# Running the two 64-row tiles of the TensorE array out of phase, with PSUM in single banks

## The chip, the cores and the metric

The kernel runs on one core of one Trainium2 chip. Times are device microseconds of that core. "Before" is 742.64 us in the median of the three runs (742.42 to 743.63). A ratio is made from the fast runs of both kernels in the same rounds, so it isn't quite the ratio of the medians quoted beside it.

The profile's names: PE is the engine of the matmuls (TensorE) and PEld its weight loads, ACT is ScalarE, DVE VectorE, POOL GpSimd. PSUM is the memory that matmuls write into; it is used here in eight banks, each of 512 fp32 columns.

## The reference

Tokens (32768 of them, 192 features, from 8 sequences) pass through a causal convolution with 7 softmax-normalised taps for each of 8 heads, and then through two matrix products with an ELU between them:

```python
out = np.einsum('hk,bskhg->bshg', softmax(weight), x_unfolded)   # 7 taps per head
h = out.reshape(-1, 192) @ w_in                                  # 192 -> 2048
g = np.where(h > 0.0, h, np.exp(np.minimum(h, 0.0)) - 1.0)       # ELU
return (g @ w_out).astype(np.float32)                            # 2048 -> 192
```

## The kernel before

The work runs in 32 **groups** of 1024 tokens. A group has 16 **places**, one for each 128 of the 2048 hidden features. (I number them 0 to 15, and first products through all groups as n = 16 x group + place.) The array is used as two tiles of 64 rows. Everything is bf16 or fp16 into fp32 PSUM.

- **First product**: at each place, each tile takes three matmuls of 512 columns (192 = 3 x 64) for its 512 tokens, into one PSUM bank.
- **The chain behind it**: ACT takes the exponential of the bank into SBUF (E), POOL clamps it, and DVE combines E and the bank into gT (fp16). Only then is the bank free.
- **Output rounds**: 128-token by 192-column matmuls of gT with w_out. A half group takes 64 pairs of them. Each tile holds 64 of the 128 hidden features of a place, so every output sum (bank `ops[g]`) needs both tiles, first one and then the other. `turned` says which tile works on which sum. The program never lets both tiles write one bank at once: at a **tile change** the new tile waits on a semaphore for the other tile's last round.
- **Conv**: 240-column matmuls for a later group, copied to SBUF by ACT.

Before, both tiles do everything in step, as pairs, and PSUM slots are pairs of banks (three slots for first products and convs, one pair for output sums):

```python
GAPS = ((), (1,), (16,), (7,), (7,), (7,), (6,), (7, 3, 10))   # rounds after each first product; turned flips at each number
...
elif item[0] == "h":                        # one place: both tiles
    wait_slot(k)                            # DVE has combined BOTH banks of the slot's last user
    for j in range(3):
        for r in range(2):
            ins = pe.matmul(H[:, k % 3, GS * r : GS * (r + 1)], w_in[...], att[...],
                            start=(j == 0), stop=(j == 2), tile_position=(HP * r, 0))
    ins.then_inc(s_h)
else:                                       # rounds: both tiles, each on its own sum
    ...
        if runs[prev][0][1] != turned:
            W(s_swap, 2 * (prev + 1))       # tile change
    ...
        for rt in range(2):
            g = rt ^ turned
            ins = pe.matmul(acc[:, g, d0 : d0 + D], gT[HP * rt : HP * (rt + 1), ...], w_out[...],
                            tile_position=(HP * rt, 0))
```

ACT copies output sum 0 and DVE output sum 1 at the end of each half group.

## Time and profile before

| | before |
|---|---|
| median | 742.64 us |
| one group in the middle of the run | 22.40 us |
| the same, if both tiles streamed without a gap | 21.74 us |
| busy: PE, DVE, ACT, POOL | 98, 89, 86, 89% |

The group time is the mean distance of the first first-product of group 3 from that of group 30, over 27 groups. The second row comes from the start times of single matmuls in the trace. Within a tile, a first product follows another after 216 ns, a round after 82.5 ns and a conv matmul after 102 ns. A group has 48, 128 and 8 of them per tile: 10.36 + 10.57 + 0.82 = 21.74 us.

The page of the kernel before, parts 1 and 5 (line, engine, operation, tiles, count | busy us, mean ns | idle time just before, and what ended most of it):

```profile
PE 730.1 (98%) x11866; PEld 502.6 (68%) x11866; DVE 657.3 (89%) x1106; ACT 636.4 (86%) x1224; POOL 663.7 (89%) x1108
...
L583 DVE SCALAR_TENSOR_TENSOR gT<-E,H 128x512 f16<-128x512 f32 x1024 | 622.1, 681 | 68.4 <-POOL E L431 68.1
...
L513 ACT ACTIVATE E<-H 128x512 f32<-128x512 f32 x1024 | 542.9, 602 | 72.2 <-PE H L733 39.3
...
L773 PEld LDWEIGHTS ops<-w_out,gT 64*128 64x128 f16 x8064 | 343.9, 94 | 117.7 <-issue 14.4
...
L733 PEld LDWEIGHTS H<-att,w_in 64*128 64x128 bf16 x3072 | 131.9, 94 | 105.2 <-DVE gT L583 30.6
...
L473 ACT ACTIVATE osb<-ops 128x384 f32<-128x384 f32 x63 | 31.3, 497 | 9.5 <-PE ops L773 9.5
L575 DVE COPY osb<-ops 128x384 f32<-128x384 f32 x63 | 34.6, 549 | 4.6 <-PE ops L773 4.6
```

Who waited for whom from 52 to 697 us, the stretch without start and tail (us in total, times, longest):

```profile
PEld H L733 <- DVE gT L583: 25.4, 58, 0.4
...
PEld ops L773 <- PE ops L773: 7.5, 50, 0.2
```

The windows view of four groups (length, then each engine's busy us):

```profile
core 0: us, PE busy (x) PEld busy (x) DVE busy (x) ACT busy (x) POOL busy (x), PEclk, DMA share, GB/s
300.00:389.60 89.60, 89.60 (x1476) 62.05 (x1472) 81.43 (x136) 79.10 (x153) 82.23 (x138) 1.00 0.47 79
```

PE sets the pace here: it is busy for the whole window, and no other engine is. "Busy" hides the gaps, though. A matmul's recorded end is modelled (243 ns for a round, 376 ns for a first product), so the next one nearly always starts inside it. The single start times give the gaps: 22.40 - 21.74 = 0.66 us a group. They lie where first products wait for DVE to free a slot (0.41 us a group, at places 4, 6, 12, 14 and 0), and where rounds change tiles behind a conv (a step of 151 ns instead of 102; 0.17 us a group). The two lines of the waits view are these two (the view counts from the weight load, and only what the modelled ends leave open, so its sums are smaller).

### The profile page before, as it was taken

The page shows a single profiled execution, that of the slowest core. Times are in us where ns is not written, and L with a number is a line of the kernel's source. Part 1 is how long each engine was busy: PE and PEld are TensorE (multiplying, and loading weights), DVE is VectorE, ACT ScalarE, POOL GpSimd, SP SyncE. Part 2 cuts the span into 40 slices and gives each one's busy share as a digit, 9 for nine tenths or more (in the row PEclk, how much of TensorE's full clock was granted, in tenths as well). Part 3 has the DMA queues.
Part 4 walks back from the last instruction along what each step waited for, and adds up shares of the span by engine and source line. Part 5 has one row for each costly group of instructions (what it writes and reads, how often), then busy time and mean ns, then how long its engine had stood idle before and what let it go on. Part 6 is the DMA issues. An engine that isn't in the chain of part 4 may idle for free.

```text
span 741.6 us, 28196 instructions
## 1 busy us (share of the span) xinstructions
PE 730.1 (98%) x11866; PEld 502.6 (68%) x11866; DVE 657.3 (89%) x1106; ACT 636.4 (86%) x1224; POOL 663.7 (89%) x1108
## 2 busy tenths in 40 slices
PE   8799999999999999999999999999999999999998
PEld 4467666667667667666667666666676676666666
DVE  4889889889889889899899898898898898898895
ACT  5888898888888888888888888888888988988883
POOL 7899999999999999999999999999999999998883
PEclk9999999999999999999999999999999999999999
DMA  9554524544535535435535435545345445343201
GB/s 168 95 85 83 94 43 89 94 67 87 76 58 94 94 60 96 68 62 95 95 61 94 57 75 94 89 65 94 49 83 95 70 84 94 43 88 81 68 24 65
DMA packets 131858, 58.94 MB, mean 79 GB/s; under 512 B 96020, under 2 KB 131348, under 8 KB 131732
## 3 DMA queue, kind: packets, MB, share of 16 engines
q0 software_dynamic: 43136, 17.28, 24.1%
q1 hardware_dynamic: 88308, 39.37, 20.4%
q8 instruction: 93, 1.52, 0.8%
q10 hardware_dynamic: 288, 0.49, 0.2%
q14 instruction: 33, 0.27, 0.2%
HBM read 35.61 MB, written 25.17 MB: 82 GB/s over the span
## 4 chain that ended last, share of the span: by engine, by line
PE 94%; DMA 3%; POOL 1%; ACT 0%; DVE 0%; issue 0%
PE ops L773 45%; PE H L733 45%; PE H L701 3%; DMA w_in<-in_moe_w_in_dram 1%; DMA w_in<-w_in 1%; PE H L773 1%; POOL E L431 1%; POOL w_in L386 1%; POOL xg L381 0%; DVE gT L583 0%; ACT E L513 0%; DMA wh<-in_weight_dram 0%; ACT csb L483 0%; DVE osb L575 0%
## 5 line engine op out<-in xcount | busy, mean ns | idle before, releaser
L583 DVE SCALAR_TENSOR_TENSOR gT<-E,H 128x512 f16<-128x512 f32 x1024 | 622.1, 681 | 68.4 <-POOL E L431 68.1
L431 POOL TENSOR_SCALAR E<-E 128x512 f32<-128x512 f32 x1024 | 603.5, 613 | 65.7 <-ACT E L513 57.8
L513 ACT ACTIVATE E<-H 128x512 f32<-128x512 f32 x1024 | 542.9, 602 | 72.2 <-PE H L733 39.3
L773 PE MATMUL ops<-w_out,gT 64*128 64x192 f16 x8064 | 428.2, 243 | 1.8 <-ACT csb L483 1.2
L773 PEld LDWEIGHTS ops<-w_out,gT 64*128 64x128 f16 x8064 | 343.9, 94 | 117.7 <-issue 14.4
L733 PE MATMUL H<-att,w_in 64*128 64x512 bf16 x3072 | 409.5, 377 | 3.8 <-DVE gT L583 2.1
L733 PEld LDWEIGHTS H<-att,w_in 64*128 64x128 bf16 x3072 | 131.9, 94 | 105.2 <-DVE gT L583 30.6
L483 ACT ACTIVATE csb<-H 128x480 bf16<-128x480 f32 x118 | 60.9, 568 | 12.6 <-PE H L701 12.6
L381 POOL DMA_DIRECT2D xg<-in_x_dram x62 | 55.2, 890 | 0.1
L701 PE MATMUL H<-xg,Tm 64*128 64x240 bf16 x472 | 44.4, 263 | 0.0
L473 ACT ACTIVATE osb<-ops 128x384 f32<-128x384 f32 x63 | 31.3, 497 | 9.5 <-PE ops L773 9.5
L575 DVE COPY osb<-ops 128x384 f32<-128x384 f32 x63 | 34.6, 549 | 4.6 <-PE ops L773 4.6
L701 PEld LDWEIGHTS H<-xg,Tm 64*128 64x128 bf16 x472 | 18.0, 93 | 3.7 <-issue 1.2
L773 PE MATMUL H<-w_out,gT 64*128 64x192 f16 x128 | 5.9, 243 | 0.0
L386 POOL DMA_DIRECT2D w_in<-in_moe_w_in_dram x7 | 4.9, 697 | 0.6 <-DMA wh<-in_weight_dram 0.6
L773 PEld LDWEIGHTS H<-w_out,gT 64*128 64x128 f16 x128 | 5.3, 94 | 0.0
L608 PE MATMUL ops<-zw 128*128 128x512 bf16 x9 | 4.0, 631 | 1.2 <-DVE zw L525 1.2
L483 ACT ACTIVATE csb<-ops 128x480 bf16<-128x480 f32 x6 | 3.5, 588 | 0.0
L608 PEld LDWEIGHTS ops<-zw 128*128 128x128 bf16 x9 | 1.2, 143 | 3.2 <-issue 1.9
L561 DVE CAST att<-H 128x512 bf16<-128x512 f32 x1 | 0.7, 692 | 3.0 <-PE H L664 3.0
L701 PE MATMUL ops<-xg,Tm 64*128 64x240 bf16 x24 | 2.3, 266 | 1.0 <-ACT csb L483 0.8
L701 PEld LDWEIGHTS ops<-xg,Tm 64*128 64x128 bf16 x24 | 0.8, 94 | 2.8 <-ACT csb L483 1.3
(49 smaller groups left out, 30.8 us busy)
## 6 DMA issues: line engine op xcount, KB each, us to landing
out_dram<-osb SPq DMA_DIRECT2D x126, 192.0 KB, 4.8
xg<-in_x_dram POOLq DMA_DIRECT2D x61, 240.0 KB, 5.2
w_in<-in_moe_w_in_dram POOLq DMA_DIRECT2D x4, 192.0 KB, 6.8
w_out<-in_moe_w_out_dram POOLq DMA_DIRECT2D x1, 768.0 KB, 15.1
att<-csb SPq DMA_TRANSPOSE x31, 6.2
xf<-in_x_dram ACTq DMA_DIRECT2D x1, 384.0 KB, 3.2
xf<-in_x_dram SPq DMA_DIRECT2D x1, 384.0 KB, 3.8
w_in<-in_moe_w_in_dram POOLq DMA_DIRECT2D x1, 288.0 KB, 10.9
```

The lines of the kernel that those rows point to most:

```text
L381: g.dma_start(xg[:, b, v0 : v0 + whole, :], src).then_inc(s_x[b][part - 1], 16)
L386: g.dma_start(w_in[HP * r : HP * (r + 1), :, c0:c1], moe_w_in.rearrange("(p j) f -> p j f", j=3)[:, :, c0:c1],).then_inc(s_w[k], 16)
L431: g.tensor_scalar(out=E[:, n % NE, u, :], in0=E[:, n % NE, u, :], scalar1=1.0, scalar2=0.0, op0=ALU.min, op1=ALU.max,).then_inc(s_clp)
L473: a.activation(*out_pieces(key, 0), ACT.Copy).then_inc(s_oev)
L483: return a.activation(csb[:, s % 2, :].rearrange("p (j v h i) -> p h j v i", j=3, v=2 * WPG, h=HEADS)[:, h0 : h0 + HB], conv_bank(m)[:, b, ...
L513: a.activation(E[:, n % NE, u, :], H[:, k, GS * u : GS * (u + 1)], ACT.Exp).then_inc(s_exp)
L575: v.tensor_copy(*out_pieces(key, 1)).then_inc(s_od)
L583: v.scalar_tensor_tensor(out=gT[:, s % NG3, q, u, :], in0=E[:, n % NE, u, :], scalar=1.0, in1=H[:, slot_of_pair[n] % 3, GS * u : GS * (u + ...
L608: pe.matmul(ops[:, 0, :], zw[:, 0:P], zw[:], start=True, stop=True)
L701: ins = pe.matmul(to[:, b, n1 * hh : n1 * (hh + 1)], Tm[HP * rt : HP * (rt + 1), h, :], xg[HP * rt : HP * (rt + 1), s % NXB, :, :].rearran ...
L733: ins = pe.matmul(H[:, k % 3, GS * r : GS * (r + 1)], w_in[HP * r : HP * (r + 1), j, 2 * FC * (q // 2) + q % 2 : 2 * FC * (q // 2 + 1) : 2 ...
L773: ins = pe.matmul(acc[:, g, d0 : d0 + D], gT[HP * rt : HP * (rt + 1), t % NG3, q, g, t0 : t0 + P], w_out[HP * rt : HP * (rt + 1), q, :], s ...
```

## The change

The intent: use banks one by one instead of in pairs, and let one tile do its first product while the other does rounds, so that banks are asked for, filled and freed evenly. The order is planned: each tile gets its own list with planned times (216, 83 and 236 ns per item), and the two lists are merged by time into one program. Tile changes fall to three a group. ACT now makes all output copies (except at the very end). Core of the diff, with cuts:

```diff
-LAG = -5
-GAPS = ((), (1,), (16,), (7,), (7,), (7,), (6,), (7, 3, 10))
+LAG = -4
+ROUNDS = (
+    ((0, (0, 17)), (1, (6, 4, 7, 11, 4)), (0, (15,))),
+    ((0, (0, 14, 8, 10)), (1, (4, 10, 5, 13))),
+)
-CONV_AT = ((2, 1, 1), (10, 2, 0))
+CONV_AT = ((2, 1, 1, 0), (8, 1, 1, 1), (12, 2, 0, 0), (15, 2, 0, 1))
+M_NS, R_NS, C_NS = 216, 83, 236
...
+    tiles, at = ([], []), [0, 0]
+    def put(rt, ops_of):
+        cost = {"h": M_NS, "o": R_NS, "c": C_NS, "w": M_NS}
+        for op in ops_of:
+            tiles[rt].append((at[rt], rt, len(tiles[rt]), op))
+            at[rt] += cost[op[0]]
     for n in range(NP):
...
+        for u in range(2):
+            rt = 1 - u
+            beside = [("c", 2 * cs + g - 2, b, u) for cs, g, b in convs]
+            beside += [single(item, rt) for item in rounds_at.get(n, ())]
+            put(u, [("h", n, u, j) for j in range(3)])
+            put(rt, beside)
+        if n % 2:
+            at[:] = [max(at)] * 2
+    steps.extend(op for *_, op in sorted(tiles[0] + tiles[1], key=lambda v: v[:3]))
...
-                    W(s_tt, 2 * was[1] + 2)
+                    W(s_tt, 2 * was[1] + was[2] + 1)
...
+                    elif steps[seen[acc]][2] != rt:
+                        W(s_swap[1 - rt], ends_run[seen[acc]])
```

At each place, then, tile 0 does first product, then rounds; tile 1 does rounds, then first product. The numbers in `ROUNDS` are rounds per tile at successive places, with `turned` in front. Tile changes come at places 14, 3 and 8; only place 8 has a conv in front of its rounds.

## The prediction

> **What bounds it now.** The tensor engine: the page has PE busy 98% of 741.6 us and the chain of waits is 94% PE; DVE, POOL and ACT are at 89, 89 and 86%. From 300 to 389.6 us (windows view) PE is busy for all 89.60 us, DVE 81.4, POOL 82.2, ACT 79.1. A group of 1024 tokens takes 22.4 us (chain in order of time: pieces 11.2 us apart, half a group each).
>
> By the start times of single matmuls in the trace, a pair of first products (512 columns, both tiles) takes 216 ns, a pair of output rounds (192) 82.5, a conv pair (240) 102. A group has 48, 128 and 8: 10.36 + 10.57 + 0.82 = 21.74 us. So the tiles already stream back to back; about 0.65 us a group, 20 us in all, can be won (floor near 722). That slack is first products waiting for DVE to free a PSUM slot (about 0.4 us a group, after the two places where ACT idles 1.1 us for an unfinished output sum), and rounds that change tiles just after a conv (steps of 151 ns instead of 102, about 0.15 us).
>
> **What the change does.** Same matmuls. It takes away (1) pairing: six banks turn singly, and ACT can start after one tile's three matmuls; (2) most tile changes of the sums: 3 a group, not 16; (3) the ACT bubble before the output copy. It moves 62 copies from DVE (549 ns each) to ACT (497 ns; +31 us; ACT then about 21 of 22 us a group).
>
> It adds an exposure. Tile 1 starts a token group with rounds just after tile 0 ended the last one with rounds, so at a tile change the wait is bare. Before, three first products (648 ns) covered it. The trace shows its length: 316 ns from the last round's start to the first changed round, across a conv; less the 82.5 ns step, 233 ns. The queue is in order, so the other tile is held too. Two of three changes have no conv in front: about 0.5 us a group. Planned times that differ from real ones (conv 236 against 204) may cost 0.1; banks where a conv takes one of six, 0.1 to 0.3.
>
> So 0.65 us goes and 0.5 to 0.8 comes back: nearly a wash. Start and tail should move by under 2 us.
>
> **Can the tiles run unlike lengths?** The Trainium skill, "TensorEngine Tiling (Array Packing)", Key Properties, says tiles operate independently; "TensorE: Matmul & The Clock Gate", Part 3, says matmuls start and end in strict program order. The trace agrees with the first as far as it goes: where tile 1 lags by 21 ns, a round of tile 0 starts while tile 1's 512-column matmul still streams. A short matmul overtaking a long one is nowhere in it.
>
> **Prediction.** 738 us, 8 in 10 within 722 to 756. Faster by over 2%: 0.17; within 2%: 0.70; slower by over 2%: 0.13.
>
> **Shown right by:** steps per tile still 216 and 82.5 ns; first products wait clearly less for DVE; new stalls of 0.2 to 0.3 us twice a group, PE waiting for PE ahead of "ops"; ACT busy near 667 us, DVE near 622; no ACT wait of 1 us ahead of "osb"; a group 22.1 to 22.5 us.
>
> **Made wrong by:** a short matmul that can't pass a long one (rounds slow down, over 5% slower); ACT becoming the limit (first products wait, a group above 22.6 us); tile changes that hide (near 725).

## More of the kernel before

The waits for DVE come just after the places where ACT makes three copies in a row and serves no first product (the timeline of ACT, start us and length):

```profile
297.68 1.03 ACT L483 ACTIVATE csb<-H 128x480 bf16<-128x480 f32 x2 [0.21 <-PE H L701]
298.60 0.50 ACT L473 ACTIVATE osb<-ops 128x384 f32<-128x384 f32 x1
299.22 2.06 ACT L513 ACTIVATE E<-H 128x512 f32<-128x512 f32 x4
```

## The result and the profile after

741.19 us in the median of four runs (740.13 to 741.40), against 743.13 for the kernel before in the same rounds: ratio 0.9965, 95% interval 0.9947 to 0.9982. It is faster by a third of a per cent. Of the span's 2.3 us, the 27 groups in the middle gave 0.4 us (22.388 us a group, against 22.403) and start and tail the rest.

The page after, the same lines:

```profile
PE 730.8 (99%) x11878; PEld 648.1 (88%) x11878; DVE 649.3 (88%) x1044; ACT 665.9 (90%) x1286; POOL 666.7 (90%) x1108
...
L588 DVE SCALAR_TENSOR_TENSOR gT<-E,H 128x512 f16<-128x512 f32 x1024 | 642.6, 683 | 74.4 <-POOL E L447 69.0
...
L519 ACT ACTIVATE E<-H 128x512 f32<-128x512 f32 x1024 | 573.4, 605 | 52.0 <-PE H L727 42.0
...
L759 PEld LDWEIGHTS ops<-w_out,gT 64*128 64x128 f16 x8064 | 537.1, 94 | 41.0 <-PE ops L759 24.9
L727 PEld LDWEIGHTS H<-att,w_in 64*128 64x128 bf16 x3072 | 259.1, 94 | 29.0 <-DVE gT L588 7.9
...
L489 ACT ACTIVATE osb<-ops 128x384 f32<-128x384 f32 x125 | 61.0, 488 | 10.2 <-PE ops L759 5.9
...
L580 DVE COPY osb<-ops 128x384 f32<-128x384 f32 x1 | 0.6, 557 | 4.5 <-PE ops L759 4.5
```

The waits from 52 to 697 us, and the same window of 89.6 us:

```profile
PEld ops L759 <- PE ops L759: 22.6, 87, 0.4
PEld H L727 <- DVE gT L588: 1.2, 4, 0.5
```

```profile
300.00:389.60 89.60, 89.47 (x1473) 80.68 (x1475) 80.16 (x129) 82.82 (x161) 82.70 (x138) 1.00 0.48 79
```

One wait was traded for another. First products waited 25.4 us for DVE; now 1.2. Rounds waited 7.5 us for rounds of the other tile; now 22.6, in 87 waits, which is three a group for 29 groups.

To see what the waits cost each tile, I took every matmul's start from the trace and gave it to its tile: the records don't name the tile, so I matched them to the two tiles' lists in their order, such that no tile starts a matmul sooner than the 216, 82.5 or 102 ns of the one in front. What is left over is idle time of that tile. It sums to 647 ns a group for each tile: 22.39 - 21.74. For tile 1, 585 of these are at the three tile changes: 263 ns at place 3, 263 at place 14, 59 at place 8 behind the conv. Tile 0 loses as much: some 360 ns because the same waits hold it, 141 at place 5, where its first round of a half group waits for ACT's copy of the sum before (the round starts 47 ns after the copy's signal), and 76 at place 0.

One tile change of the kernel after, place 14, as the timeline of PE shows it (start, length, operation):

```profile
255.54 0.38 PE L727 MATMUL H<-att,w_in 64*128 64x512 bf16 x1
255.56 0.24 PE L759 MATMUL ops<-w_out,gT 64*128 64x192 f16 x1
255.65 0.38 PE L727 MATMUL H<-att,w_in 64*128 64x512 bf16 x1
256.02 0.25 PE L759 MATMUL ops<-w_out,gT 64*128 64x192 f16 x1
256.03 0.39 PE L727 MATMUL H<-att,w_in 64*128 64x512 bf16 x1
256.11 0.33 PE L759 MATMUL ops<-w_out,gT 64*128 64x192 f16 x2
```

And the same instructions with tile and position in the program, by the matching just described (ns of idle time of the tile in front):

```
255.480 us  program  -2  tile 0  round                  idle     0
255.540 us  program  -3  tile 1  first product 173.2    idle     0
255.562 us  program  -1  tile 0  round (last of run)    idle     0
255.645 us  program  +0  tile 0  first product 174.0    idle     0
256.019 us  program  +1  tile 1  round (tile change)    idle   263
256.029 us  program  +4  tile 0  first product 174.1    idle   168
256.112 us  program  +2  tile 1  round                  idle    10
256.195 us  program  +3  tile 1  round                  idle     0
```

Three things are to be seen here. First, the tiles do run unlike lengths side by side at full pace: away from the waits the steps stay 216 and 82.5 ns. Second, matmuls don't start in program order: first product 174.1 stands behind two rounds of tile 1 (+2 and +3) and starts before both. Of the 11784 matmuls from the first group on, about 3700 start after one that stands behind them in the program, at most three positions. Third, the changed round starts 457 ns after the last round of the run (255.562), not after the 316 ns that the prediction took from the kernel before. But it starts 479 ns after tile 1's **own** last first product (255.540), and this is so at all three tile changes of a group (medians of 28 or 29: 479, 479, 479), while the distance from the last round is 473, 399 and 464 ns.

That suggests **theory A**: an instruction's semaphore signal isn't given before those of the matmuls ahead of it in the program. First product 173.2 is at program position -3 and the last round at -1; by theory A the round's signal has to wait for the long matmul's. The trace can be asked directly: it holds the time of every semaphore update (no view of `prof` lists them; these are read from the packed trace). Here the long matmul gives its signal at 255.930, 390 ns after its start. The last round gives its own at 255.972, 42 ns later and 410 ns after its own start, where a round with nothing unfinished ahead of it gives it after 257. The changed round starts 47 ns after that signal. All 1600 signals of PE in this run come in program order; by their usual delays (257 ns for a round, 277 for a conv, 390 for a first product) 156 of them would not. In the kernel before, a change waits for the last rounds of both tiles, whose signals come 34 ns apart; it starts 333 or 334 ns after the second of the two rounds in 71 of 114 cases across a conv, and 316 is the shortest. **Theory B** is the plain one of the prediction: a tile change costs a fixed time after the last round, whatever the order. **Theory C** is that ACT, which went from 86 to 90% busy, sets the pace now, and the stalls at tile changes only fill time.

### The profile page after: what moved, and what is told of

It reads as the page before. It is cut to its first block, busy times and chain, and to the rows that moved or that the text cites. A ratio compares the mean times of both kernels' runs of the same rounds, so it can differ in the third digit from the quotient of the medians.

```text
span 739.3 us, 28636 instructions
## 1 busy us (share of the span) xinstructions
PE 730.8 (99%) x11878; PEld 648.1 (88%) x11878; DVE 649.3 (88%) x1044; ACT 665.9 (90%) x1286; POOL 666.7 (90%) x1108
## 4 chain that ended last, share of the span: by engine, by line
PE 95%; DVE 2%; POOL 1%; ACT 1%; DMA 1%; issue 0%; SPq 0%; ACTq 0%
PE ops L759 49%; PE H L727 42%; PE H L703 2%; DVE gT L588 2%; POOL E L447 1%; PE H L759 1%; ACT E L519 1%; DMA xf<-in_x_dram 1%; PE H L660 0%; PE ops L660 0%; PE H L640 0%; DVE xh L554 0%; ACT csb L497 0%; POOL xg L397 0%; PE H L628 0%
## 5 line engine op out<-in xcount | busy, mean ns | idle before, releaser
L588 DVE SCALAR_TENSOR_TENSOR gT<-E,H 128x512 f16<-128x512 f32 x1024 | 642.6, 683 | 74.4 <-POOL E L447 69.0
L727 PE MATMUL H<-att,w_in 64*128 64x512 bf16 x3072 | 626.2, 376 | 1.4 <-DVE gT L588 0.6
L519 ACT ACTIVATE E<-H 128x512 f32<-128x512 f32 x1024 | 573.4, 605 | 52.0 <-PE H L727 42.0
L759 PE MATMUL ops<-w_out,gT 64*128 64x192 f16 x8064 | 619.1, 243 | 0.6
L759 PEld LDWEIGHTS ops<-w_out,gT 64*128 64x128 f16 x8064 | 537.1, 94 | 41.0 <-PE ops L759 24.9
L727 PEld LDWEIGHTS H<-att,w_in 64*128 64x128 bf16 x3072 | 259.1, 94 | 29.0 <-DVE gT L588 7.9
L703 PE MATMUL H<-xg,Tm 64*128 64x240 bf16 x496 | 90.7, 263 | 0.9 <-DVE gT L588 0.9
L489 ACT ACTIVATE osb<-ops 128x384 f32<-128x384 f32 x125 | 61.0, 488 | 10.2 <-PE ops L759 5.9
L703 PEld LDWEIGHTS H<-xg,Tm 64*128 64x128 bf16 x496 | 43.4, 94 | 11.2 <-issue 1.1
L580 DVE COPY osb<-ops 128x384 f32<-128x384 f32 x1 | 0.6, 557 | 4.5 <-PE ops L759 4.5
```

What stands on the lines that cost most here:

```text
L489: a.activation(*out_pieces(acc), ACT.Copy).then_inc(s_oev)
L519: a.activation(E[:, n % NE, u, :], bank_of(op[:3]), ACT.Exp).then_inc(s_exp)
L588: v.scalar_tensor_tensor(out=gT[:, s % NG3, q, u, :], in0=E[:, n % NE, u, :], scalar=1.0, in1=bank_of(op[:3]), op0=ALU.subtract, op1=ALU.m ...
L703: ins = pe.matmul(bank_of(op[:3])[:, n1 * hh : n1 * (hh + 1)], Tm[HP * rt : HP * (rt + 1), h, :], xg[HP * rt : HP * (rt + 1), s % NXB, :, ...
L727: ins = pe.matmul(bank_of(op[:3]), w_in[HP * r : HP * (r + 1), j, 2 * FC * (q // 2) + q % 2 : 2 * FC * (q // 2 + 1) : 2,], att[HP * r : HP ...
L759: ins = pe.matmul(to[:, d0 : d0 + D], gT[HP * rt : HP * (rt + 1), t % NG3, q, g, t0 : t0 + P], w_out[HP * rt : HP * (rt + 1), q, :], start ...
```

## The experiments

All kernels gave correct results. "Group" is the time of one group, as above.

| run | median us | ratio to before, 95% interval | group us |
|---|---|---|---|
| before | 743.13 | | 22.403 |
| after | 741.19 | 0.9965 (0.9947 to 0.9982) | 22.388 |
| lag100 | 740.50 | 0.9965 (0.9950 to 0.9979) | 22.377 |
| lag160 | 729.61 | 0.9814 (0.9800 to 0.9829) | 22.053 |
| lag300 | 737.34 | 0.9916 (0.9902 to 0.9931) | 22.276 |
| coarse | 733.29 | 0.9869 (0.9852 to 0.9885) | 22.149 |
| more_turns | 763.35 | 1.0273 (1.0257 to 1.0288) | 23.135 |
| conv_swap | 741.09 | 0.9971 (0.9956 to 0.9986) | 22.398 |
| dve_copy | 847.58 | 1.1399 (1.1382 to 1.1416) | 25.898 |
| in_phase | 779.86 | 1.0496 (1.0477 to 1.0515) | 23.753 |
| in_phase_gaps | 784.24 | 1.0544 (1.0526 to 1.0562) | 23.888 |
| conv_late | 755.09 | 1.0151 (1.0136 to 1.0167) | 22.871 |
| lag160_conv | 741.61 | 0.9972 (0.9954 to 0.9991) | 22.440 |
| lag200_conv | 741.79 | 0.9973 (0.9957 to 0.9989) | 22.442 |

### more_turns: more of the suspected cost

```diff
-    ((0, (0, 14, 8, 10)), (1, (4, 10, 5, 13))),
+    ((0, (0, 14, 8)), (1, (10, 4)), (0, (10,)), (1, (5, 13))),
```

> Five tile changes a group instead of three, by ordering the rounds of the second half 14, 8 | 10, 4 | 10 | 5, 13; the change that stood behind a conv (59 ns) is now bare, and two more bare ones are added. If a bare tile change costs 263 ns: (263-59) + 2 x 263 = 730 ns a group, 31 groups: 761 to 766 us. If tile changes aren't what costs (ACT or banks do): 738 to 746 us.

Measured: 763.35 us, inside the expected 761 to 766. Tile 1 stalls five times a group, 262 ns each, 1311 of its 1394 idle ns. The waits view, 52 to 697 us:

```profile
PEld ops L759 <- PE ops L759: 50.6, 140, 0.5
PEld H L727 <- DVE gT L588: 6.0, 31, 0.5
```

So a bare tile change does cost its 0.26 us, and PE's stalls add to the time one for one. This also gives a second look at the release: the changed rounds start 399 to 551 ns (medians of the five places) after the last round, but 478 ns after tile 1's own last first product, at all five.

### lag100, lag160, lag300: is it order or time?

Tile 1's planned clock starts late, and the two clocks aren't set equal again. Nothing else changes, not even the amount of work at any place:

```diff
-    tiles, at = ([], []), [0, 0]
+    tiles, at = ([], []), [0, 160]
...
-        if n % 2:
-            at[:] = [max(at)] * 2
```

With 100 ns, tile 1's last first product before a tile change is still ahead of tile 0's last round in the program (planned 116 ns before the change of place, against 83). With 160 it is behind it (56 against 83).

> Tile 1's planned clock starts 100 ns late. Theory A (signals are given in program order): the last round's signal waits for tile 1's own last first product, which still stands before it in program order, so the changed round still starts 479 ns after that product's start, and the stall stays 263 ns, twice a group: no change, 739.5 to 743 us. Theory B (the wait is a fixed time after the last round's start): tile 1 is free 100 ns later, so each stall shrinks by 100: 31 groups x about 0.25 us less, 732 to 735 us.

> As lag100 with 160 ns, which is just enough to put tile 1's last first product behind tile 0's last round in program order. Theory A: a jump against lag100; the wait falls to 316 ns after the last round's start, the stall to 0 to 90 ns: 31 groups x about 0.45 us less, 725 to 730 us. Theory B: a small further step from lag100, 730 to 733 us.

> As lag100 with 300 ns. Both theories A and B: the stall at tile changes is gone or below 50 ns (about 0.55 us a group, 17 us): 722 to 727 us, unless banks or ACT then set the pace, in which case waits of first products for DVE, or of ACT copies, show up and it stays above 730 us.

Measured: 740.50, 729.61 and 737.34 us. From "after" to lag100 the stalls stay (255 ns at places 3 and 14). The 60 ns from 100 to 160 give 11 us. In lag160 the changed round starts 303 ns after the last round (both places), and no longer 479 ns after tile 1's first product (386 and 284). This is what A said and B can't give: the wait depends on what stands ahead in the program. The recorded signals agree. In lag160 the last round gives its signal 257 ns after its start, at both places, and the changed round starts 47 ns later. In each of the 13 runs since the change, PE gives 1600 signals or more, and not one out of program order. The waits view of lag160 has them less than half as long:

```profile
PEld ops L757 <- PE ops L757: 9.5, 51, 0.2
PEld H L725 <- issue: 5.8, 29, 0.2
```

lag160 does the same ACT work as the changed kernel and is 1.6% faster (medians 729.61 and 741.19 us, from different rounds), so theory C falls: ACT didn't set the pace at 741 us. What is left in lag160 is 312 ns a group: 166 and 66 ns for tile 1 at the tile changes at places 3 and 14. Tile 0 meets them with one wait of 162 ns at place 0, whose first product starts 147 ns after the end of the DVE combine that frees the bank (the "issue" line above, once a group). Elsewhere a first product that waits for a bank starts 56 to 61 ns after it. Only the first product of place 0 also waits for the transposed conv result, and there the trace shows a wait instruction of its own (EVENT_SEMAPHORE, 51 ns) ahead of it. So some 90 of the 162 ns seem to be the cost of the second wait and not of the bank, and so with the 76 ns of the changed kernel at place 0, where the 147 ns are the same; no run tests that. The whole wait falls on tile 0 alone and takes from tile 1's lag, which is why the lag at place 3 is only some 50 ns (303 less the round's own 82.5 less the stall of 170 in those places where it stalls).

lag300 missed: I expected 722 to 727 us. Its tile changes are cheap (13 ns), but tile 0's wait at place 0 grew to 223 ns and holds tile 1 by 161, and new stalls come at the places with a conv: tile 0's conv half waits 85 ns at place 8, and tile 1's rounds are held 60 to 70 ns at places 2, 8 and 15. The waits, 52 to 697 us:

```profile
PEld H L725 <- issue: 7.6, 29, 0.3
PEld H L701 <- PE H L701: 6.5, 29, 0.2
```

A conv's second half waits for a signal of its first half, which runs on the tile that lags. With a lag above 216 ns the first half stands behind tile 0's second first product in the program, and I first took its signal to come late by theory A, as the expectation of lag200_conv below still says. The recorded signals don't bear that out: the signal comes 277 ns after the start of the conv's last matmul, as in the changed kernel. The first half itself is late. At place 8 of lag300 its last matmul starts 412 ns after tile 0's first product; 277 for the signal and 46 to the start of the second half make 735 ns, and tile 0 is ready after 3 x 216 = 648. In lag200_conv that last matmul starts after 311 ns, its signal is there at 588, and there is no stall.

### coarse: how strict is program order?

```diff
-M_NS, R_NS, C_NS = 216, 83, 236
+M_NS, R_NS, C_NS = 83, 83, 83
```

> The plan that interleaves the tiles takes 83 ns for every matmul, so program order is a first product, a round, a first product, a round, a first product, then rounds only. If a matmul can't start before those ahead of it in program order: the fourth round waits for the third first product (432 instead of 249 ns), about 0.18 us a token group and tile phase, 1024 of them: over 60 us slower. If each tile has its own queue that runs ahead by three matmuls or more, as the trace of the changed kernel suggests: within 15 us.

Measured: 733.29 us, faster than the careful plan. Here about 4600 matmuls start after one that stands behind them, by up to five positions, and the steps in each tile stay 82.5 and 216 ns. So each tile runs on through its own matmuls, some positions ahead of the other, and the fine interleaving of the plan isn't needed. It is faster because this order happens to put tile 1's last first product behind the last round, as in lag160: the stalls at places 3 and 14 are 13 and 48 ns. That is theory A a second time, without any lag: at both places the changed round starts 47 ns after the recorded signal.

### conv_swap: cover for the bare tile changes

```diff
-CONV_AT = ((2, 1, 1, 0), (8, 1, 1, 1), (12, 2, 0, 0), (15, 2, 0, 1))
+CONV_AT = ((3, 1, 1, 0), (8, 1, 1, 1), (12, 2, 0, 0), (14, 2, 0, 1))
```

> Convs moved from places 2 and 15 of a group to 3 and 14, in front of the bare tile changes. Stalls 263 -> 59 ns twice a group: 0.41 us x 31 = 12.6 us less, 726 to 732 us. If ACT or banks set the pace: 738 to 745 us.

Measured: 741.09 us, a miss. The cover works (20 ns of stall at place 3, 0 at place 14), but the time came back at place 14 as a wait of 475 ns of the conv itself, for a bank:

```profile
PEld H L703 <- DVE gT L588: 20.9, 57, 0.5
...
PEld ops L759 <- PE ops L759: 4.7, 29, 0.2
```

The conv matmuls (L703) now wait for DVE. A conv takes one of the six banks in turn, and this one follows tile 0's first product of place 12, whose combine ends 3.0 us after its last matmul starts, against 2.4 us at best, because ACT makes output copies just ahead of it.

### dve_copy: were the copies on ACT a cost or a need?

```diff
-    on_dve = {acc for acc, x_ in final.items() if x_ >= tail_from and acc[3] == 1}
+    on_dve = {acc for acc in final if acc[3] == 1}
```

> The output copies of one half of the tokens go back to DVE (undoes that part of the change): ACT busy about 635 us, DVE about 684 us. If PE's stalls at tile changes set the pace: no change, 739 to 743 us. If ACT at 90% does (rival): faster by 3 us or more, below 738 us.

Measured: 847.58 us. Neither theory's number came: both looked only at how busy the engines are. The waits, 52 to 697 us:

```profile
PEld ops L759 <- DVE osb L580: 92.0, 50, 2.0
PE ops L759 <- DVE osb L580: 76.5, 50, 1.7
```

The copy takes 0.55 us on DVE and 0.49 on ACT, but it starts at another time. On ACT in the changed kernel it starts 0.28 us (tile 1's sum) to 0.98 us (tile 0's) after the sum's last round. On DVE it starts 2.5 to 2.9 us after it, and the next half group's first round waits 1.7 to 1.9 us. DVE comes last in the chain exponential, clamp, combine: its combine of a bank ends about 2.4 us or more after the last matmul into that bank has started. The copy stands behind the combines of earlier first products in DVE's order. ACT comes first in that chain and reaches the copy about two steps earlier. With one empty place between half groups, the copies on ACT come in time and those on DVE don't; in this plan the moved copies are a necessary part of the change.

### in_phase, in_phase_gaps: is the phase shift needed, or are single banks enough?

Both keep single banks, few tile changes and copies on ACT, but each tile does its first product and then its rounds:

```diff
-            put(u, [("h", n, u, j) for j in range(3)])
-            put(rt, beside)
+            first = [op for op in beside if op[0] == "c" and rt]
+            put(rt, first)
+            put(rt, [("h", n, rt, j) for j in range(3)])
+            put(rt, [op for op in beside if op not in first])
```

in_phase_gaps also takes a pacing like the old one: `LAG = -5` and `((0, (0, 1, 16)), (1, (7, 7, 7, 11)), (0, (15,)))` for both halves.

> Single banks, few tile changes and copies on ACT are kept; the two tiles run in step again (first products of both, then rounds of both). Three first products cover every tile change, so its stalls are gone. If the single banks took away the waits of first products: 722 to 728 us. If it was the phase shift that spread the bank use and hid the output copies: waits for DVE of 0.2 to 0.4 us a group come back, 729 to 737 us.

> in_phase with the pacing of the kernel before (0, 1, 16, 7, 7, 7, 11, 15 rounds in each half, one place earlier): single banks, 2 to 3 tile changes a half, copies on ACT, tiles in step. If in_phase lost to its uneven pacing alone: 722 to 735 us. If tiles in step ask for banks two at a time and single banks alone don't cure that: waits for DVE of 0.4 us a group or more, 738 to 755 us.

Measured: 779.86 and 784.24 us, slower than either theory said. No stall is left at tile changes (three first products cover each), but first products wait for DVE again (in_phase, 52 to 697 us):

```profile
PEld H L729 <- DVE gT L590: 70.7, 136, 1.9
PE H L729 <- DVE gT L590: 34.0, 55, 1.5
```

Tile 1's first product at place 13 alone waits 1.1 us in in_phase and 1.4 us in in_phase_gaps. In the changed kernel tile 1 does its 17 rounds of place 13 (1.4 us) before that first product, and the bank is free by then. So in this plan it is the phase shift, and not the single banks alone, that removes the bank waits; single banks in step are worse than pairs were with their own plan. These runs don't tell how well an in-step plan with single banks could do if its convs and rounds were tuned for it.

### conv_late, lag160_conv, lag200_conv: towards the best version

The conv at place 15 costs lag160 its wait at place 0. I moved the convs to places where the trace shows banks freed long before they are needed:

```diff
-CONV_AT = ((2, 1, 1, 0), (8, 1, 1, 1), (12, 2, 0, 0), (15, 2, 0, 1))
+CONV_AT = ((4, 1, 0, 1), (6, 1, 1, 0), (8, 1, 1, 1), (12, 2, 0, 0))
```

> The changed kernel with its convs moved from places 2, 8, 12, 15 of a group to 4, 6, 8, 12, where the trace shows that a bank's release comes 0.5 us and more before it is needed; no lag. The 76 ns wait of tile 0 for a bank at place 0 goes, but tile 1's stalls at the tile changes (263, 59, 263 ns) set the pace: 739 to 742.5 us. If the bank waits count beside them: 736 to 738.5 us.

> lag160 with the convs moved as in conv_late. In lag160 the bank wait of 162 ns at place 0 falls on tile 0 alone and eats the lag, so tile 1 stalls 166 ns at place 3 and 66 at place 14. Without it the lag stays 160 and the stalls are 233 - 160 = 73 ns each at places 3 and 14: 311 -> 180 to 220 ns a group, 3 to 4 us less than lag160: 725 to 727 us.

> As lag160_conv with 200 ns: stalls of 233 - 200 = 33 ns each; still under 216 ns, so that a conv half's signal doesn't wait for the second first product of the other tile (which I think cost lag300 its conv stalls of 60 to 87 ns): 722.5 to 725 us. If conv stalls come back: above 727 us.

Measured: 755.09, 741.61 and 741.79 us, all misses. As expected, the wait at place 0 is gone in all three. As expected, the tile changes get cheap with a lag: 36 and 62 ns at places 3 and 14 in lag160_conv, 28 and 41 in lag200_conv (expected 73 and 33 each). What I overlooked is one new wait at place 6, where the conv waits for a bank: 483, 531 and 529 ns of tile 1's time. conv_late, 52 to 697 us:

```profile
PEld ops L759 <- PE ops L759: 25.6, 85, 0.5
PEld H L703 <- DVE gT L588: 18.7, 28, 0.7
```

My reading of spare time was taken with no conv in that stretch. The banks are a ring of six. A conv put into it makes every first product that follows it within the ring wait for a bank that was filled one turn later, and two convs within three places do it twice. The spare half microsecond was the very one that the conv then used.

The fastest kernel measured is therefore lag160: 729.61 us, 0.9814 of the kernel before. It beats both kernels.

## Why the prediction was right, point by point

The time was right: 738 us with 722 to 756 was said, 741.19 came, and "nearly a wash" was the point. The accounts beneath it held in the main, but not in all parts.

- **What bounds it, and how much is to be won.** Held. 0.65 us a group of slack was said, 0.66 is there by the group time.
- **Waits for banks go.** Held: 25.4 to 1.2 us. But the reason given, that ACT idles 1.1 us for an unfinished output sum twice a group, was wrong. I had read it in the last groups. The page lists 9.5 us of such idle time in all, and there is none from 52 to 697 us. In the steady stretch ACT isn't idle there; it makes three copies in a row. That the banks are late because of these copies is argued from their place in the trace; no run shows it by itself.
- **Tile changes are bare.** Held, and more_turns shows the price. The size was off: 233 ns was said for a bare one (and so about 30 behind a conv of 204), 263 and 59 were measured. The step that failed is "316 ns from the last round's start". The release isn't counted from the last round but from tile 1's own last first product, which is ahead of it in the program: 479 ns, of which 432 to the round's signal. lag100 and lag160 show that the order decides. (316 was also the shortest of the steps in the kernel before; most were 333 or 334.)
- **The other tile is held too.** Held in part: tile 0's next first product is 168 to 194 ns late, not 263.
- **0.1 for the plan's wrong times, 0.1 to 0.3 for banks.** Too much. Tile 0 waits 76 ns at place 0, perhaps for more than the bank (see lag160), and would have to wait for tile 1 anyway; the rest is about 60 ns a group. The larger tile changes made up for it: 0.5 to 0.8 us was said to come back, and 0.65 did. So it is partly luck that the sum came out: one term was too small and the others too large.
- **Loads.** ACT near 667 us was right (665.9). DVE near 622 was not: 649.3. Taking the copies off gave 34 us, but the combines' busy time rose from 622.1 to 642.6 us at nearly the same mean (681 and 683 ns): they come singly more often, and overlap less in the record.
- **What the moved copies are for.** Missed. I costed them as load only; dve_copy shows that they set when the next half can start, worth 106 us (847.58 against 741.19).

## What to carry to other kernels

When one engine's queue feeds two concurrent streams, look at what stands ahead of a signalling instruction in the program, in the other stream too: a short one behind a long one signals late, and moving the long one behind it can be worth more than the redesign (here 11 us for 60 ns of planned lag). A rotation of buffers has no spare place to be found in a trace without the new user in it: each new user makes all that follow wait for a later release. And ask of a small copy not only how long it takes on an engine but how far behind that engine runs.

## What the Trainium skill lacked or had wrong

- "TensorE: Matmul & The Clock Gate", Part 3, The mechanism, says that matmuls keep strict program order in start and end. Across the two row tiles the starts here do not: about 3700 of 11784 in the changed kernel begin after one that stands behind them (up to three positions), and up to five positions in coarse, with correct results. The ends aren't recorded but modelled; the signals, which are recorded, do come in program order, all 1600 of them in the changed kernel, as the page's order of ends would have it.
- "TensorEngine Tiling (Array Packing)", Key Properties, says that tiles operate independently. It lacks what that is worth with unlike lengths: 512-column and 192-column matmuls side by side keep 216 and 82.5 ns a step. It also lacks that a semaphore wait of one tile holds the other, whose matmul stands behind it in the program (168 to 194 ns here).
- "Trainium Kernel Development and Optimization", Performance Expectations, calls LDWEIGHTS busy % a good measure of the distance to the roofline. The busy share of PEld in these profiles can't serve as that measure: it went from 68 to 88% with nearly the same loads (11866 and 11878, 94 ns each) and 0.35% less time, because it counts loads that overlap once, and in step more of them overlap. The summed time of the loads is 151% of the span in both kernels; how to read a sum above 100%, with two row tiles, the page lacks.
- No page that I read has the delay from DVE's combine to the first product that takes its bank: 56 to 61 ns from the combine's recorded end, in all runs where a first product waited for that alone.
